# Two recurrent attention layers and their dense layers on one core: late values computed groups ahead, the last quarter of heads in two halves, weights on one queue, and a planner with an urgency per kind of operation

## The chip, the cores and the metric

The kernel runs on one core of one Trainium2 chip. The metric is the device time of one execution in microseconds (us), lower is better. The median of 3 runs of the kernel before is 1724.3 us (1722.43 to 1724.99). The times of the profiled executions are spans of the trace, about 1.8 us shorter than the time of the same run, except for e9 and e17 below: their kept traces span 1725.4 and 1672.1 us, where the profiled run on record took 1727.4 and 1668.4 us, so they show another execution.

## The reference

Two layers are applied in turn, twice: a recurrent attention with memory, then a dense layer. Cut to what matters:

```python
def A(x, mem, Wq, Wk, Wv, Wo):           # 64 segments of 32 tokens, one after the other
    for s in range(64):
        h = concat([mem, x[32*s : 32*s+32]])          # 8 memory rows + 32 tokens = 40 rows
        q, k, v = h @ Wq, h @ Wk, h @ Wv              # 32 heads of 128
        p = softmax(mask(q @ k.T / sqrt(128)))        # 40 x 40 for each head
        o = (p @ v) @ Wo                              # sum over the heads, 40 x 512
        mem = o[:8]                                   # the next segment waits for this
        outs.append(o[8:])

def B(x, w1, w2): return relu(x @ w1) @ w2            # 512 -> 1376 -> 512

x = x + A(layernorm(x)); x = x + B(layernorm(x))      # layer 1
x = x + A(layernorm(x)); x = x + B(layernorm(x))      # layer 2, same weights
```

x is 2048 x 512 in bf16. The memory makes a segment wait for the one before it: q and k, scores, softmax, the transposition of P, attend, projection, and then the memory rows for the next q and k.

## The kernel before: the parts that matter

All weights lie in on-chip memory. Both layers run at once, layer 2 four segments behind layer 1. I call the work on segment k of layer 1 and segment k-4 of layer 2 "step" k; there are 68 steps. What one step does has a fixed list of operations, and a planner in Python fixes at build time in which order each engine runs them. It simulates the engines with a cost for each operation, takes the operation of highest priority among those that can start, computes from the plan how late each operation may start, makes that the new priority, and repeats; the best of 60 randomly varied passes is used.

```python
# the planner, before (cut)
for n in range(PASSES):                                     # 60
    if n > 5:
        look, stay = best[3:]
        look, stay = abs(look + rnd.gauss(0, 0.05)), abs(stay + rnd.gauss(0, 0.2))
    total = self.forward(prio, look, stay)                  # list scheduling, gives an order
    late = self.backward(total)                             # latest starts become priorities
    ...
```

An operation can be bound to one engine, or be offered to two (`copy_op`: ACT or DVE). A matmul uses the full array or half of it (`tile=COL64`, two halves then run side by side).

Each step has four quarters of 8 heads:

```python
for p in range(4):
    qk = [queries_keys(k, hg, a_lo, a_hi) for hg in (2 * p, 2 * p + 1)]
    PTs.append(scores(k, p, a_lo, a_hi, qk))
for p in range(4):
    attend(k, p, a_lo, a_hi, PTs[p])
project(k, act, seg)
```

`scores` is a chain: products (PE), then mask, maximum, subtract (DVE), exp (ACT), sum, reciprocal (DVE), P = e * 1/sum (POOL), transposition (PE), and two copies of the transposed P, rows 0 to 63 and rows 64 to 127 of one PSUM bank, to `PT`, each on ACT or DVE:

```python
for b in range(2):
    def keep(eng, b=b):
        R = slice(64 * b, 64 * b + 64)
        copy_on(eng, PT[R, a_lo:a_hi, :, b, :]..., tp[R, ...]...)
    copy_op(n, keep, r=[tp, "zero PT"], w=[PT, (PT, b)] if b == 0 else [(PT, b)])
```

The values v = h @ Wv are computed in the step for the second half of layer 1's tokens and all of layer 2 (`vw`). The values of the first 16 tokens of each layer-1 segment do not depend on the memory: they are computed for a group of four segments at once (I call them "late values"; four pieces of 8 half-array matmuls of 512 columns), in the step before the group starts, and copied by DMA into place for each segment:

```python
def late_values(g):
    ...                                            # gather x of 4 segments into XG
    values(XG[:, :, :], vg, "vg", ["XG"])          # 4 pieces, PE 0.86 us each
...
if 0 in seg and seg[0] % GS == GS - 1 and seg[0] // GS + 1 < NG:
    late_values(seg[0] // GS + 1)                  # just before it is needed
```

The weights arrive in 1 MB pieces, in pairs on two queues (SP's and POOL's), w1 and w2 right behind them:

```python
pairs = (("q0", "k0"), ("q1", "k1"), ("v0", "v1"), ("q2", "k2"), ("v2", "v3"), ("q3", "k3"), ("o0", "o1"), ("o2", "o3"))
for i, pair in enumerate(pairs):
    for (c, pc), (eng, q) in zip(pair, ((SP, nc.sync), (POOL, nc.gpsimd))):
        ...
```

## Time and profile before

| | before |
|---|---|
| time, median of 3 runs | 1724.3 us |
| PE busy | 95% of the span |
| step 1 starts at | 68.9 us |
| four-step period in the middle | 25.4, 24.2, 25.9, 24.7 us |

How to read it. "PE busy" says little here, because a matmul's record is longer than its spacing (a product of 80 columns is recorded as 0.20 us long, and the next one starts 0.036 us later), so that the records cover short waits. I use another measure all through this document. The "floor" of a stretch is what its matmuls take at the best spacing that the trace shows: 36 ns from start to start for 80 columns, 25 ns for 40 (half of each where two half arrays run side by side), 108 ns for one of 512 columns in half-array pairs, plus 96 ns for every change between full and half array (408 of them). The rest of the stretch is "idle". Before: floor 1584.4 us and idle 138.1 us, of it 50.3 us until step 1 starts, 6.4 us in steps 1 to 3, 15.4 us in steps 4 to 19, 53.1 us in steps 20 to 63, and 12.9 us at the end.

The floor rests on spacings that fit the Trainium skill, "TensorE: Matmul & The Clock Gate", section "Back-to-back issue gap": its isolated gap of N/2.4 + 2.5 ns is 35.8 ns for 80 columns and 216 ns for 512, and this trace shows 36 ns and 216 ns per pair. The same section's sustained figure for matmuls with weight loads, 81 ns at 128 columns, is not what this kernel shows: each of its 80-column products has its own weight load and they still follow each other at 36 ns.

From the page of the kernel before, parts 1, 2 and 4 (busy time by engine; granted PE clock and DMA rate in 40 slices of the span; the chain of waits by engine):

```profile
PE 1632.0 (95%) x40536; PEld 1402.1 (81%) x40536; DVE 909.6 (53%) x2294; ACT 1096.3 (64%) x2657; POOL 357.8 (21%) x873
PEclk8799999999999999999999999999999999999999
GB/s 352 132 22 18 19 18 22 16 21 19 17 20 18 22 18 20 19 18 20 18 22 17 20 19 18 19 18 22 18 19 20 17 16 18 20 15 18 17 6 6
PE 86%; DVE 4%; ACT 3%; SPq 2%; POOL 1%; DMA 1%; issue 1%; ACTq 0%; POOLq 0%; DVEq 0%
```

The work is PE's, but the first slice shows the load of the weights and a lowered clock. The chain of waits of the kernel before, from 25 to 75 us (start, length, what):

```profile
25.59 17.23 SPq L365
...
42.86 15.53 DMA w_sb<-in_B_w_dram
...
59.89 2.13 DMA V_88<-vw
...
66.48 2.15 PE st_124 L876 x64
...
68.65 0.20 DVE HT_80 L892
...
68.89 0.69 PE work_122 L732 x16
```

SP's sequencer sits on the issue of Wo until 42.8 us, the load of w1/w2 takes the engines until 58.4 us, and V's pieces queue up behind it, so that the first step's attention ends, and step 1 starts, at 68.9 us.

One four-step period of the kernel before (steps 32 to 35), as busy time of each engine in each step; the columns are PE, PEld, DVE, ACT, POOL (with instructions), granted PE clock, share of DMA, GB/s:

```profile
830.70:856.10 25.40, 23.45 (x599) 20.93 (x598) 12.78 (x32) 16.37 (x38) 5.47 (x14) 1.00 0.08 19
856.10:880.30 24.20, 23.89 (x601) 20.75 (x598) 13.92 (x34) 17.40 (x43) 6.01 (x14) 1.00 0.10 25
880.30:906.20 25.90, 25.84 (x628) 22.25 (x629) 13.58 (x34) 16.64 (x39) 4.44 (x10) 1.00 0.08 17
906.20:930.90 24.70, 24.70 (x602) 20.59 (x599) 14.45 (x34) 16.22 (x39) 5.40 (x13) 1.00 0.07 16
```

The first step of the four has a floor of 22.4 us and loses 3.0 us. Why is seen in the timeline of its last 10 us (start, length, engine, line, operation, and in brackets the idle time before it and what ended it):

```profile
846.11 0.23 PE L849 MATMUL work_122<-PT_102,V_88 128*64 128x80 bf16 x2 [0.98 <-ACT PT_102 L640]
...
848.77 0.42 ACT L640 CAST PT_103<-work_121 64x320 bf16<-64x320 f32 x1 [0.32 <-PE work_121 L481]
849.22 0.49 DVE L642 CAST PT_103<-work_121 64x320 bf16<-64x320 f32 x1 [0.37 <-ACT PT_103 L640]
849.77 0.20 PE L849 MATMUL work_122<-PT_103,V_88 128*128 128x80 bf16 x1
...
850.10 0.99 POOL L814 TENSOR_TENSOR P_85<-es_101,sm_110 128x160 bf16<-128x160 f32 x2 [1.01 <-DVE sm_110 L798]
...
851.15 0.32 PE L481 MATMUL work_123<-ident,P_85 128*128 128x80 bf16 x4 [0.33 <-POOL P_85 L814]
```

The last quarter's P takes POOL 0.99 us, its transposition waits for that, and the two copies of a transposed P run one after the other (DVE waited for ACT's). The largest wait, 1.2 us from start to start less the floor, ends at 846.11 us, in the first line shown: attend waits there for the PT of an earlier quarter, whose second copy, on ACT, also came after the first.

### The profile page before, as it was taken

To read this page: it belongs to the slowest core of one execution; us is meant where nothing else is said; L and a number is where in the kernel's file an instruction comes from. 1 tells how busy PE (TensorE), PEld (TensorE's weight loads), DVE (VectorE), ACT (ScalarE), POOL (GpSimd) and SP (SyncE) were. 2 spreads that over 40 slices of the span, in tenths; PEclk is the share of its full clock that TensorE was granted. 3 is DMA by queue.
4 is the path that set the end of the run, shared out by engine and by line. 5 is a ranking of instruction groups with operands and counts; after the bars stand their busy time and mean duration, and the time that the engine had idled before them with its cause. 6 is when DMAs were issued, how large, how long until landed. Compare 5 with 4: busy or idle time off the path is not lost.

```text
span 1722.5 us, 89836 instructions
## 1 busy us (share of the span) xinstructions
PE 1632.0 (95%) x40536; PEld 1402.1 (81%) x40536; DVE 909.6 (53%) x2294; ACT 1096.3 (64%) x2657; POOL 357.8 (21%) x873
## 2 busy tenths in 40 slices
PE   2699999999999999999999999999999999999998
PEld 2578888888888888888888888888888888888886
DVE  4345556555555655555565555556555555554554
ACT  1366666666666666666666666666666666666664
POOL 3121222122112212221222222122212212211211
PEclk8799999999999999999999999999999999999999
DMA  9400000000000000000000000000000000000000
GB/s 352 132 22 18 19 18 22 16 21 19 17 20 18 22 18 20 19 18 20 18 22 17 20 19 18 19 18 22 18 19 20 17 16 18 20 15 18 17 6 6
DMA packets 31008, 50.54 MB, mean 29 GB/s; under 512 B 8248, under 2 KB 14400, under 8 KB 30624
## 3 DMA queue, kind: packets, MB, share of 16 engines
q1 hardware_dynamic: 27632, 34.54, 7.9%
q0 software_dynamic: 2560, 9.80, 1.5%
q8 instruction: 317, 5.19, 1.3%
q10 hardware_dynamic: 432, 0.47, 0.1%
q14 instruction: 67, 0.55, 0.1%
HBM read 21.70 MB, written 2.10 MB: 14 GB/s over the span
## 4 chain that ended last, share of the span: by engine, by line
PE 86%; DVE 4%; ACT 3%; SPq 2%; POOL 1%; DMA 1%; issue 1%; ACTq 0%; POOLq 0%; DVEq 0%
PE st_124 L876 15%; PE fill_125 L684 8%; PE fill_126 L684 7%; PE work_122 L732 7%; PE work_120 L732 7%; PE work_123 L732 7%; PE work_119 L732 7%; PE work_121 L732 7%; PE fill_125 L481 6%; PE fill_126 L481 4%; SPq L365 1%; SPq L368 1%; POOL P_85 L814 1%; DMA w_sb<-in_B_w_dram 1%; PE work_119 L759 1%
## 5 line engine op out<-in xcount | busy, mean ns | idle before, releaser
L732 PEld LDWEIGHTS <-Wq_sb 128*128 128x128 bf16 x8704 | 336.0, 100 | 32.8 <-issue 19.1
L876 PE MATMUL st_124<-OT,Wo_sb 128*128 128x80 bf16 (+1 forms) x8704 | 345.7, 200 | 0.7 <-ACT OT L640 0.6
L732 PEld LDWEIGHTS <-Wk_sb 128*128 128x128 bf16 x8704 | 336.0, 100 | 1.3 <-issue 0.8
L876 PEld LDWEIGHTS <-Wo_sb 128*128 128x128 bf16 x8704 | 319.1, 100 | 10.8 <-issue 6.8
L814 POOL TENSOR_TENSOR P_82<-es_100,sm_107 128x160 bf16<-128x160 f32 (+1 forms) x136 | 57.2, 442 | 758.3 <-ACT qT_93 L640 299.5
L849 PEld LDWEIGHTS <-V_88 128*64 128x64 bf16 (+1 forms) x1488 | 89.6, 107 | 45.1 <-issue 34.6
L640 ACT CAST vw<-fill_125 128x512 bf16<-128x512 f32 x134 | 78.0, 582 | 61.8 <-PE fill_125 L684 61.7
L640 ACT CAST vw<-fill_126 128x512 bf16<-128x512 f32 x132 | 76.9, 583 | 49.3 <-PE fill_126 L684 49.2
L481 PEld LDWEIGHTS <-w_sb 128*128 128x128 bf16 (+2 forms) x1752 | 89.7, 104 | 5.3 <-issue 4.8
L814 POOL TENSOR_TENSOR P_84<-es_100,sm_109 128x160 bf16<-128x160 f32 (+1 forms) x136 | 61.8, 476 | 135.8 <-DVE sm_109 L798 103.4
L773 DVE TENSOR_TENSOR es_100<-work_121,maskb 128x320 f32<-128x320 f32 (+1 forms) x38 | 18.5, 487 | 133.7 <-PE work_121 L759 133.7
L684 PEld LDWEIGHTS <-HT_79 128*64 128x64 bf16 x1088 | 55.0, 110 | 39.6 <-issue 0.7
L849 PEld LDWEIGHTS <-vw 128*64 128x64 bf16 (+1 forms) x1480 | 82.1, 106 | 5.6 <-issue 1.9
L481 PE MATMUL fill_125<-w_sb,hT_118 128*64 128x512 bf16 (+1 forms) x645 | 85.8, 380 | 0.0
L684 PEld LDWEIGHTS <-HT_80 128*64 128x64 bf16 x1088 | 54.1, 110 | 37.8
L814 POOL TENSOR_TENSOR P_85<-es_101,sm_110 128x160 bf16<-128x160 f32 (+1 forms) x136 | 59.1, 455 | 112.2 <-DVE sm_110 L798 95.7
L773 DVE TENSOR_TENSOR es_100<-work_119,maskb 128x320 f32<-128x320 f32 (+1 forms) x37 | 17.4, 469 | 122.3 <-PE work_119 L759 118.1
L792 ACT ACTIVATE es_100<-es_100 128x320 f32<-128x320 f32 (+1 forms) x136 | 61.9, 455 | 24.6 <-DVE es_100 L786 22.4
L684 PE MATMUL fill_125<-Wv_sb,HT_79 128*64 128x512 bf16 x560 | 72.9, 382 | 0.2 <-ACT vg L640 0.2
L684 PE MATMUL fill_126<-Wv_sb,HT_80 128*64 128x512 bf16 x560 | 72.3, 380 | 0.0
L814 POOL TENSOR_TENSOR P_83<-es_101,sm_108 128x160 bf16<-128x160 f32 (+1 forms) x136 | 59.3, 458 | 49.0 <-DVE sm_108 L798 45.7
L684 PE MATMUL fill_125<-Wv_sb,HT_80 128*64 128x512 bf16 x528 | 68.2, 380 | 0.0
(364 smaller groups left out, 3902.3 us busy)
## 6 DMA issues: line engine op xcount, KB each, us to landing
V_88<-vw SPq DMA_DIRECT2D x252, 48.0 KB
V_88<-vg SPq DMA_DIRECT2D x252, 32.0 KB
Wq_sb<-in_A_Wq_dram SPq DMA_DIRECT2D x4, 1024.0 KB
Wk_sb<-in_A_Wk_dram POOLq DMA_DIRECT2D x4, 1024.0 KB, 16.2
Wv_sb<-in_A_Wv_dram SPq DMA_DIRECT2D x2, 1024.0 KB
Wv_sb<-in_A_Wv_dram POOLq DMA_DIRECT2D x2, 1024.0 KB, 18.9
Wo_sb<-in_A_Wo_dram POOLq DMA_DIRECT2D x2, 1024.0 KB, 32.6
Wo_sb<-in_A_Wo_dram SPq DMA_DIRECT2D x2, 1024.0 KB
```

What stands on the lines that cost most here:

```text
L365: q.dma_start(out=Wo_sb[:, hs, :], in_=A_Wo.rearrange("h e d -> e h d")[:, hs, :])
L368: q.dma_start(out=W_s[c][:, :, cs], in_=W_v[c][:, :, cs])
L481: nc.tensor.matmul(out_[u:v, :], lhsT=lhsT[:, u:v], rhs=rhs, start=start, stop=stop, tile_position=(0, u))
L640: nc.scalar.copy(out=out_, in_=in_)
L684: nc.tensor.matmul(vp[64 * b:64 * b + 64, :], lhsT=cols[:, c4, :], rhs=Wv_sb[:, c4, n * 512:(n + 1) * 512], start=(c4 == 0), stop=(c4 == N ...
L732: nc.tensor.matmul(qp[:, hi * 2 * L:hi * 2 * L + n], lhsT=W_sb[:, c4, h * Dh:(h + 1) * Dh], rhs=HT[:, c4, c0:c1], start=(c4 == 0), stop=(c ...
L759: nc.tensor.matmul(v[64 * g2:64 * g2 + L, a, b, ii, :], lhsT=qT[:, hi, a * L:(a + 1) * L], rhs=kT[:, hi, a * L:(a + 1) * L], start=True, s ...
L773: nc.vector.tensor_tensor(out=esv(), in0=spv(), op=ALU.add, in1=maskb[:, a_lo:a_hi, :].unsqueeze(2).to_broadcast([128, na, 4, L]))
L792: nc.scalar.activation(out=e, in_=e, func=ACTF.Exp, scale=SCALE)
L814: nc.gpsimd.tensor_tensor(out=o, in0=e, in1=s.unsqueeze(3).to_broadcast([128, na, 2, L]), op=ALU.mult)
L849: nc.tensor.matmul(o[u:u + cols, :, a, :], lhsT=V[:, p, hh * Dh + u:hh * Dh + u + cols], rhs=PT[:, a, hh, :, :], start=True, stop=True, ti ...
L876: nc.tensor.matmul(wo[:, 2 * W * c4 + c0:2 * W * c4 + c1], lhsT=Wo_sb[:, h, c4 * 128:(c4 + 1) * 128], rhs=OT[:, h, c0:c1], start=(h == 0 a ...
```

## The change

Its intent: (1) all weights on one queue (POOL's) in 2 MB pieces, v first, w1/w2 held back; (2) late values computed groups ahead and kept in HBM, groups 1 to 4 while the weights still load, in the space of w1/w2; the layernormed x too; (3) the last quarter of heads split into two halves, so that the recurrence's last softmax is half as long, and P's product offered to POOL or DVE; (4) the planner: three passes, no random search, a table of urgencies, and a rule for work that is spare. The core of the diff:

```diff
+UNITS = ((0, (0, 1)), (1, (0, 1)), (2, (0, 1)), (3, (0,)), (3, (1,)))
-PASSES = 60
+PASSES = 3
+RULE = (0.045, 0.734, 51.008, 20.581)
+AHEAD = {
+    "attend.ev": 0.03, "attend.mm": -1.07, "dense_layer.mm": -0.93, ...
+    "scores.keep": -13.15, "scores.mul": -5.63, "scores.total": 20.81, "values.mm*": -37.11, ...
+}
 ...
+            t, o = min((c for c in starts if c[0] <= lo + look), key=rank)
+            if e == PE and o.spare:
+                soon = [c for c in starts if t < c[0] < t + o.cost and prio[c[1].seq] < prio[o.seq] - far]
+                if soon: ...                       # leave the slot to the one that is due soon
 ...
-        pairs = (("q0", "k0"), ("q1", "k1"), ("v0", "v1"), ...)
+        for i, part in enumerate(("v0", "v2", "q0", "k0", "q2", "k2", "o0", "o2")):
+            ...                                    # 2 MB each, all on nc.gpsimd
+    def prepare_group(g):
+        ...                                        # load x, layernorm, xh[g] to HBM
+        late_values(g, xnT)
-        values(XG[:, :, :], vg, "vg", ["XG"])
+        if 1 <= g <= EARLY:
+            room = (w1_sb, w2_sb)[(g - 1) // 2][:] ...
+        values(XG[:, :, :], room, name, ["XG"])
+        def put():
+            nc.sync.dma_start(out=vh[g][:], in_=room[:, :, :])
+        plan.op(SP, 0.78, put, r=["loaded", ...], w=[("vh", g)], lag=4.0)
 ...
-            plan.op(POOL, t_pool(n // 2), mul, r=[es, sm], w=[("P", p, b)])
+            plan.op((POOL, DVE), (t_pool(2 * na * L), t_dve(2 * na * L)), mul, r=[es, sm],
+                    w=[("P", p, b, x) for b in range(b0, b1) for x in xs])
 ...
+    for g in range(1, NG):
+        prepare_group(g)
+    load_dense()
-        for p in range(4):
-            qk = [queries_keys(k, hg, a_lo, a_hi) for hg in (2 * p, 2 * p + 1)]
-            PTs.append(scores(k, p, a_lo, a_hi, qk))
+        for p, xs in UNITS:
+            heads = heads_of(p, xs)
+            qk = [queries_keys(k, p, heads[j:j + 4], a_lo, a_hi) for j in range(0, len(heads), 4)]
+            PTs.append(scores(k, p, xs, a_lo, a_hi, qk))
```

"loaded" is a time in the planner's picture.

## The prediction

> **What bounds it.** TensorE: matmuls cover 95% of the span (page, part 1); the chain of waits is 86% PE. I split PE time into a "floor" (every matmul at the best spacing the trace shows: 36 ns for 80 columns, 25 ns for 40, 216 ns for 512, 108 ns each where two half arrays run together, plus 96 ns for each change between full and half array) and the rest, "idle". Before: floor 1584 us (408 changes, 39 us of it) and idle 138 us. Idle by part, from the PE timeline: 50 us until step 1 starts at 68.9 us; 6 us in steps 1-3; 69 us in steps 4-63; 13 us in the last four steps and the tail.
>
> **Startup.** Windows 0-25 and 25-50 us show 346 and 352 GB/s: loading weights is the limit. Wo's issue sits in the queue until 42.9 us, w1/w2 follow, and step 0's attention waits for V0 pieces queued behind them (V_88<-vw landed at about 62 us), so Wo's last product ends at 68.6 us. The change puts the attention weights, v first, on one queue and holds w1/w2 back: 16.8 MB at 352 GB/s is 48 us, so an estimate of step 1 starting at 52-54 us. The Trainium skill, "DMA: Bandwidth & Descriptors", "Issuing engines are not separate DMA queues", says that DMAs from any engine run on the same 16 engines (so one queue should lose none; this trace, with two, cannot confirm it). Meanwhile PE computes early groups' late values: by the instruction order, floor before step 1 grows from 18.6 to 34.5 us. Idle there falls from 50 to about 18 us. Cold clock (0.60 and 0.72 granted at 25-75 us) may cost 2-4 us.
>
> **Steady state.** The old plan has four-step periods: steps of floor 22.4, 23.6, 25.4, 24.6 us take 25.4, 24.2, 25.9, 24.7. The first, without late values, loses 3.0 us to the recurrence (last scores, softmax, turn, attend, project, memory). Splitting the last quarter halves the last softmax's operations (VectorE about 0.49 to 0.32 us each, six in a chain) and lets projection overlap it, about 1 us shorter. Late values become filler, mostly spent by step 20. By the new order, steps 24-63 have floors of 23.3 and 22.9 us alternately, with at most about 0.5 us uncovered (projection followed directly by q/k). I estimate 0.4 us idle per step: 6 us in steps 4-19, 18 us in 20-63, against 69 us.
>
> **Cost.** Changes of array mode rise from 408 to 490, +8 us; matmul work is unchanged. VectorE gains 800 instructions (half of P's products move from POOL, halves split), +100 us of 910: it stays near 60%, off the path.
>
> **Sum.** Floor 1592 + idle 18 + 6 (steps 1-3) + 6 + 18 + 12 (end) = 1652; with some slip, 1655 us, 4% less. Range 1638-1682. Chances: faster by over 2% 0.93, within 2% 0.06, slower 0.01.
>
> **Signs.** Step 1's first q/k at 52-55 us (before 68.9). PE busy share 97% or more. Steps 24-63 take 23.3-23.8 us; steps 4-19 about 25.5. Attend's 1 us waits for PT disappear. VectorE busy about 1000 us, POOL about 240-260.
>
> **What would make it wrong.** One software queue loading slower than 352 GB/s (step 1 at 58 us or later); the recurrence still setting steps 24-63, now without late values as filler, at 24 us or more (each 0.5 us per step is 20 us); VectorE delaying evictions so that PE waits for PSUM banks; V0's late part from HBM coming late on the SP queue.

## The result

The changed kernel takes 1681.44 us (median of 4 runs, 1681.01 to 1684.49), against 1723.81 us of the kernel before in the same rounds. The ratio is 0.9758, 95% interval 0.9741 to 0.9775. The change is 2.4% faster; predicted was 4.0%. From the page after:

```profile
PE 1632.9 (97%) x40522; PEld 1396.9 (83%) x40522; DVE 1070.6 (64%) x3095; ACT 1062.2 (63%) x2665; POOL 246.6 (15%) x608
PEclk9999999999999999999999999999999999999999
GB/s 358 214 81 35 39 37 28 37 35 37 34 39 16 39 28 17 26 21 24 17 26 20 19 21 19 27 17 25 18 27 16 19 24 21 18 18 18 18 5 6
PE 81%; DVE 12%; DMA 3%; issue 2%; POOL 1%; ACT 1%; POOLq 0%; ACTq 0%; DVEq 0%
```

PE's share rose as foretold, but DVE's part of the chain rose from 4% to 12%. The sum of the prediction against the trace, all in us:

| | before | predicted | after |
|---|---|---|---|
| floor (changes of array mode) | 1584.4 (408) | 1592 (490) | 1592.3 (490) |
| idle until step 1 | 50.3 | 18 | 28.6 |
| idle in steps 1 to 3 | 6.4 | 6 | 6.0 |
| idle in steps 4 to 19 | 15.4 | 6 | 5.6 |
| idle in steps 20 to 63 | 53.1 | 18 | 35.7 |
| idle in steps 64 to 67 and after | 12.9 | 12 | 11.4 |
| sum | 1722.5 | 1652 | 1679.6 |

Two terms are off, by 10.6 and 17.7 us, and they are the whole miss. First the start. The chain of waits after, from 40 to 66 us:

```profile
8.90 48.50 DMA Wo_sb<-in_A_Wo_dram
...
57.45 0.97 PE st_161 L951 x32
58.42 0.98 PE fill_162 L757 x8
59.41 0.50 PE st_161 L951 x16
...
62.38 0.86 PE fill_163 L757 x8
63.24 0.50 PE work_156 L809 x16
```

The last half of Wo lands at 57.4 us, not at about 50; four pieces of late values (fill) and the last projections stand after it. The traffic of the first 60 us in the changed kernel, by queue (packets, MB, share of the 16 engines' time), and two of its transfers:

```profile
q0 software_dynamic: 4224, 16.78, 74.9%
q1 hardware_dynamic: 1120, 2.61, 12.0%
q10 hardware_dynamic: 1520, 1.52, 7.7%
...
vh_92<-w_sb SPq DMA_DIRECT2D x1, 512.0 KB
```

The weights are q0's 16.78 MB. Besides them 4.1 MB (3.4 MB until Wo had landed) ran on SP's and ACT's queues: late values on their way to HBM, x, layernormed x, pieces of V. From the packets: while q0 was nearly alone (5 to 20 us) it moved 1.9 to 2.05 MB in each 5 us; from 25 us on, with the others, 1.3 to 1.8.

Then the steady state. Steps 40 to 43 of the changed kernel, columns as before:

```profile
1019.10:1042.70 23.60, 23.57 (x613) 21.51 (x614) 14.21 (x43) 16.77 (x41) 2.23 (x5) 1.00 0.07 18
1042.70:1067.00 24.30, 23.67 (x586) 19.88 (x584) 16.86 (x45) 14.53 (x38) 4.27 (x10) 1.00 0.12 30
1067.00:1090.50 23.50, 23.50 (x612) 21.47 (x613) 14.22 (x43) 16.67 (x41) 2.22 (x5) 1.00 0.08 18
1090.50:1114.80 24.30, 23.72 (x586) 19.95 (x583) 16.76 (x45) 14.51 (x37) 4.21 (x10) 1.00 0.07 19
```

Even steps take 23.55 us with 0.25 us idle, odd steps 24.31 us, although their floor is the smaller one (22.87): they lose 1.44 us. The end of an odd step in the changed kernel:

```profile
1063.55 0.69 DVE L685 TENSOR_TENSOR ob_74<-xg_70,fill_162 64x512 bf16<-64x512 f32 x1
...
1064.27 0.32 DVE L703 CAST PT_139<-work_156 64x160 bf16<-64x160 f32 x1
...
1064.62 0.29 ACT L701 CAST PT_139<-work_156 64x160 bf16<-64x160 f32 x1 [0.81 <-DVE PT_139 L703]
1064.96 0.20 PE L924 MATMUL work_160<-PT_139,V_123 128*128 128x80 bf16 x1 [0.26 <-ACT PT_139 L701]
...
1066.70 0.22 DVE L967 CAST HT_80<-st_161 128x64 bf16<-128x64 f32 x1 [0.72 <-PE st_161 L951]
...
1066.98 0.71 PE L809 MATMUL work_159<-HT_80,Wq_sb 128*128 128x80 bf16 x15 [0.32 <-DVE HT_80 L967]
```

Two waits are seen. Attend waits 0.43 us (start to start, less the floor) for PT: its first copy stood behind a residual sum of 0.69 us on DVE, and its second copy, on ACT, waited for the first. And the next step's first q waits 0.48 us for the copy of the memory columns (HT_80), with no other matmul between. One more, of 0.2 us, is among the scores. (Lines of busy time hide all this: PE's record shows 23.67 us busy there.)

### The profile page after: what moved, and what is told of

Its sections match the earlier page's. It is cut to its first block, busy times and chain, and to the rows that moved or that the text cites. A ratio compares the mean times of both kernels' runs of the same rounds, so it can differ in the third digit from the quotient of the medians.

```text
span 1679.6 us, 90364 instructions
## 1 busy us (share of the span) xinstructions
PE 1632.9 (97%) x40522; PEld 1396.9 (83%) x40522; DVE 1070.6 (64%) x3095; ACT 1062.2 (63%) x2665; POOL 246.6 (15%) x608
## 4 chain that ended last, share of the span: by engine, by line
PE 81%; DVE 12%; DMA 3%; issue 2%; POOL 1%; ACT 1%; POOLq 0%; ACTq 0%; DVEq 0%
PE st_161 L951 13%; PE fill_162 L757 8%; PE fill_163 L757 8%; PE work_159 L809 7%; PE work_157 L809 7%; PE work_156 L809 7%; PE work_160 L809 7%; PE work_158 L809 6%; PE fill_163 L514 5%; PE fill_162 L514 4%; DMA Wo_sb<-in_A_Wo_dram 3%; DVE OT L703 2%; DVE ob_74 L685 1%; DVE ln_147 L522 1%; POOL P_85 L886 1%
## 5 line engine op out<-in xcount | busy, mean ns | idle before, releaser
L951 PE MATMUL st_161<-OT,Wo_sb 128*128 128x80 bf16 (+1 forms) x8704 | 354.5, 200 | 2.9 <-DMA Wo_sb<-in_A_Wo_dram 2.9
L951 PEld LDWEIGHTS <-Wo_sb 128*128 128x128 bf16 x8704 | 322.5, 100 | 24.3 <-issue 18.2
L701 ACT CAST vw<-fill_162 128x512 bf16<-128x512 f32 x115 | 67.3, 585 | 56.7 <-PE fill_162 L757 52.8
L701 ACT CAST vw<-fill_163 128x512 bf16<-128x512 f32 x103 | 60.3, 585 | 47.6 <-PE fill_163 L757 43.7
L924 PEld LDWEIGHTS <-V_123 128*64 128x64 bf16 (+1 forms) x1526 | 86.2, 107 | 4.0 <-issue 0.6
L514 PEld LDWEIGHTS <-w_sb 128*128 128x128 bf16 (+1 forms) x1496 | 86.8, 100 | 0.8 <-DVE ob_74 L685 0.5
L757 PEld LDWEIGHTS <-HT_80 128*64 128x64 bf16 x1088 | 51.3, 111 | 32.5 <-issue 2.5
L860 ACT ACTIVATE es_136<-es_136 128x320 f32<-128x320 f32 (+2 forms) x170 | 68.8, 405 | 14.0 <-DVE es_136 L856 9.6
L860 ACT ACTIVATE es_135<-es_135 128x320 f32<-128x320 f32 (+2 forms) x170 | 68.6, 403 | 14.2 <-DVE es_135 L856 6.2
L757 PEld LDWEIGHTS <-HT_81 128*64 128x64 bf16 x1088 | 51.0, 110 | 30.9 <-issue 1.0
L757 PE MATMUL fill_162<-Wv_sb,HT_81 128*64 128x512 bf16 x584 | 76.4, 384 | 0.0
L757 PE MATMUL fill_163<-Wv_sb,HT_80 128*64 128x512 bf16 x544 | 71.9, 387 | 0.0
L757 PE MATMUL fill_162<-Wv_sb,HT_80 128*64 128x512 bf16 x544 | 71.4, 385 | 0.0
L856 DVE TENSOR_TENSOR es_136<-es_136,mx_141 128x320 f32<-128x320 f32 (+2 forms) x170 | 68.9, 405 | 1.0
L853 DVE TENSOR_REDUCE mx_141<-es_136 128x8 f32<-128x320 f32 (+2 forms) x170 | 67.7, 398 | 1.8
L856 DVE TENSOR_TENSOR es_135<-es_135,mx_140 128x320 f32<-128x320 f32 (+2 forms) x170 | 68.0, 400 | 0.9
L853 DVE TENSOR_REDUCE mx_140<-es_135 128x8 f32<-128x320 f32 (+2 forms) x170 | 67.7, 398 | 1.4
L757 PE MATMUL fill_163<-Wv_sb,HT_81 128*64 128x512 bf16 x504 | 66.3, 385 | 0.0
L514 PE MATMUL fill_163<-w_sb,hT_155 128*64 128x512 bf16 (+3 forms) x376 | 54.4, 380 | 0.0
```

The costliest lines, as they stand in the source:

```text
L514: nc.tensor.matmul(out_[u:v, :], lhsT=lhsT[:, u:v], rhs=rhs, start=start, stop=stop, tile_position=(0, u))
L701: nc.scalar.copy(out=out_, in_=in_)
L757: nc.tensor.matmul(vp[64 * b:64 * b + 64, :], lhsT=cols[:, c4, :], rhs=Wv_sb[:, c4, n * 512:(n + 1) * 512], start=(c4 == 0), stop=(c4 == N ...
L853: nc.vector.tensor_reduce(out=mx[:, As], in_=es3(), axis=AX.X, op=ALU.max)
L856: nc.vector.tensor_tensor(out=es3(), in0=es3(), op=ALU.subtract, in1=mx[:, As].unsqueeze(2).to_broadcast([128, ns * na, L]))
L860: nc.scalar.activation(out=es[:, A], in_=es[:, A], func=ACTF.Exp, scale=SCALE)
```

## Experiments

Every kernel but one gave the reference's result by intent; that one is marked. "Idle" is the span less the floor of the built order. In some traces up to 9 us of matmul records are missing, so idle by step is an upper bound there, marked "at most".

| run | what it is | median us | ratio to before (95%) | idle until step 1 | idle steps 20-63 |
|---|---|---|---|---|---|
| changed kernel | | 1681.4 | 0.9758 (0.9741-0.9775) | 28.6 | 35.7 |
| e1_hold_stores | other traffic waits for Wo | 1701.5 | 0.9869 (0.9854-0.9884) | at most 48.6 | at most 37 |
| e5_early_norm | zeroing in pieces | 1680.6 | 0.9746 (0.9732-0.9761) | at most 27 | at most 38 |
| e6_stores_behind | stores behind the weights | 1682.4 | 0.9755 (0.9740-0.9769) | 26.6 | 38.4 |
| e12_add_later | one sum later on DVE | 1676.7 | 0.9726 (0.9711-0.9740) | 30.1 | 29.1 |
| e17_memory_aside | e12, no wait for the memory | 1669.9 | 0.9686 (0.9672-0.9701) | 29.2 | 27.0 |
| e14_behind_norm_add | e5, e6 and e12 together | 1668.1 | 0.9671 (0.9657-0.9686) | at most 23 | at most 29 |
| e3_spread | late values released over the steps | 1696.0 | 0.9842 (0.9824-0.9860) | at most 28 | at most 42 |
| e4_unsplit | last quarter whole | 1770.7 | 1.0271 (1.0252-1.0290) | at most 31 | at most 113 |
| e7_no_urgency | empty table | 1723.4 | 0.9989 (0.9972-1.0006) | at most 30 | at most 59 |
| e8_old_planner | old planner | 1695.4 | 0.9837 (0.9821-0.9854) | 26.6 | 36.5 |
| e9_serial_keeps | planner told of serial copies | 1727.0 | 1.0012 (0.9995-1.0029) | 30.5 | 54.3 |
| e10_old_unsplit | old planner, unsplit | 1764.6 | 1.0236 (1.0220-1.0251) | 27.7 | 119.3 |
| e15_old_spread | old planner, spread | 1714.3 | 0.9941 (0.9926-0.9956) | 28 | about 49 |
| e16_old_unsplit_spread | old planner, unsplit, spread | 1725.4 | 1.0006 (0.9991-1.0021) | 29 | 71 |

### The start

**e1_hold_stores.** SP's transfers wait for a small DMA that reads the end of Wo.

```diff
+        def gate():
+            nc.sync.dma_start(out=held[:], in_=Wo_sb[0:1, H - 1, 0:8])
+        plan.op(SP, 0.5, gate, r=[("W", "o", 2)], w=["loaded"], lag=0.0)
```

> Edit to the changed kernel: the first instruction of the SP queue is a 16-byte copy of the last Wo values to HBM, so that every SP transfer (the stores of late values, 0.5 MB each, and the x loads of groups 5 and 6) really waits until Wo has landed, as the planner believed it did. PE order unchanged (floor 1592 us, 490 mode changes). Theory A (in the changed kernel's trace about 1.7 MB of SP traffic lands before Wo, the weights' queue falls from 2.0 to 1.3-1.5 MB per 5 us): Wo lands about 4 us earlier, at 53 us instead of 57; step 1 starts at 58-60 instead of 63.2; whole kernel 2 to 4 us faster than the changed kernel, 1678 us. Rival B (one software queue is slower by itself late in the load, or HBM is): Wo lands at 57 as before, step 1 at 63, whole kernel the same or slower.

Wo landed at 51.6 us instead of 57.4, with 1.0 MB of other traffic before it instead of 3.4, and with the weights' queue at 1.5 to 2.05 MB in each 5 us: the other traffic does cost the load 6 us. (Not the whole fall of the rate is company, though: from 40 to 50 us the queue was alone in this run and still moved only 1.75 and 1.51 MB in 5 us. Why is open.) But step 1 started at 83.2 us. The waits of this run up to 90 us (who, for what: us in total, times, longest):

```profile
ACT vg L707 <- DMA held<-Wo_sb: 27.8, 1, 27.8
...
PE work L844 <- ACT kT L707: 26.1, 2, 25.9
```

ACT, which has nothing to do with the gate, waited 27.8 us for the gate's DMA. In the built program ACT's next DMA raises the same semaphore as the gate's DMA (one of eight that SP's and ACT's DMAs are given) and waits first until the gate's has landed. So the whole-kernel answer is spoilt; the landing of Wo is the answer that stands.

**e5_early_norm.** DVE's zeroing of 9 us, which held back the first layernorm, is cut into single operations.

```diff
-        plan.op(DVE, 9.5, zero_rest, w=["zero PT"] + ... + ["zero x"] + ...)
+        plan.op(DVE, 0.3, zero(p_xr.tiles), w=["zero xr"])
+        plan.op(DVE, 0.9, zero([vw]), w=[...])
+        ...                                        # one operation for each tile
```

> Edit to the changed kernel: the 9 us of zeroing on VectorE ahead of group 0's layernorm is cut into single operations, so that the planner can put the normalisation first. Theory: TensorE idles 15.2 us at the start because of VectorE, not of the weights (Wv's first part lands at about 8-9 us): with the normalisation early, the first value product starts at 9 to 11 us, the late values of groups 1-4 are done before Wo lands, step 1 starts at 59 to 61 us, and the whole is 2 to 5 us faster, near 1678. Rival: Wo's landing at 57 us alone sets step 1; the early start only moves idle time from before 15 us to between 20 and 57: step 1 at 62-63 us, the whole the same within 1 us.

PE's first values started at 10.9 us instead of 15.2, step 1 at 61.5 us instead of 63.2, and the time is the same within its interval. Wo was issued later in this order (its second half at 13.3 us instead of 8.9) and landed at 57.9 us. Of the 4.3 us that PE gained at its first values, longer waits before step 1 took back 2.7 (for Wq, for Wo, and for the copies of x to XG).

**e6_stores_behind.** The stores of groups 0 to 4 go to the weights' queue, behind them.

```diff
-            nc.sync.dma_start(out=vh[g][:], in_=room[:, :, :])
+            (nc.gpsimd if early else nc.sync).dma_start(out=vh[g][:], in_=room[:, :, :])
```

> Only the stores of the first five groups' late values move: onto the queue of the weights, behind them. Theory (the store traffic of 0.5 MB each slowed the weights, and that is the 10.7 us by which the start was longer than predicted): Wo lands at about 53 us instead of 57, step 1 starts at about 59 us instead of 63, the whole is 2 to 4 us shorter (ratio to the kernel before about 0.974). Rival (the fixed order, with its late-value pieces between the last products, and the cold clock set the start, not the load): step 1 moves by less than 1.5 us and the whole by less than 1 us.

Step 1 started at 60.1 us, idle until there 26.6 us: a part of the theory. Wo's second half landed 46.5 us after its issue instead of 48.5. The whole did not get shorter: steps 4 to 63 idle 5 us more than in the changed kernel's trace. With the planner's new order the gain was given back; by which wait is not settled. Start times also scatter: e12, whose order is the same up to step 1, started it at 64.6 us instead of 63.2. So 1 to 2 us at the start in one trace prove nothing by themselves.

### The odd steps

**e12_add_later.** The order of the changed kernel, with one edit after planning: DVE's last residual sum of a pair goes behind the copy of the last PT and the layernorm. (By the built program this moved 23 of the 32 sums, those of all odd steps from 19 to 61 and of step 65; the other nine did not stand right before that pair. The expectation speaks of 32.)

```diff
-        for o in plan.order():
+        for o in add_later(plan.order()):      # moves add1 and its store behind [scores.keep, layernorm.norm]
```

> The planner's order is kept except that in 32 pairs of segments VectorE does the last residual sum (0.69 us) after the copy of the last transposed P and the layernorm instead of before them. Theory (0.43 us of the 1.44 us that an odd step loses is this sum standing before the copy that attend waits for): odd steps 24.31 -> 23.9 us, idle 1.44 -> about 1.0, the whole about 8 us shorter (1672 to 1675 us). Rival (the wait comes back at the next link of the chain, at the copies of OT, of the layernormed x or of the memory): odd steps stay at 24.1 to 24.3, the whole moves by under 3 us.

Odd steps took 23.93 us instead of 24.31, their idle fell from 1.44 to 1.06 us, even steps stayed at 23.55: the theory, for the steps. The whole is 4.8 us shorter (median 1676.7), not 8: steps 20 to 63 gave 6.6 us, and step 4 started 3.8 us later in this trace, with nothing changed before it but chance. The end of an odd step in this run:

```profile
1064.15 0.32 DVE L722 CAST PT<-work 64x160 bf16<-64x160 f32 x1
...
1064.50 0.29 ACT L720 CAST PT<-work 64x160 bf16<-64x160 f32 x1
...
1065.12 0.20 PE L943 MATMUL work<-PT,V 128*128 128x80 bf16 x1
...
1067.19 0.28 PE L828 MATMUL work<-HT,Wq_sb 128*128 128x80 bf16 x3 [0.32 <-DVE HT L986]
```

PT's copies are no longer late (attend follows a projection without a wait), and the wait for the memory columns is as it was.

**e17_memory_aside.** As e12, and from step 8 on the memory columns are written to a tile that no product reads. This computes a wrong recurrence; the comparison still passed, so with these inputs the memory weighs less than its tolerance.

```diff
-                nc.vector.tensor_copy(out=HTn[:, :, m_lo:m_hi], in_=v(2 * W)[:, :, m_lo:m_hi])
+                if k < 8: nc.vector.tensor_copy(out=HTn[:, :, m_lo:m_hi], in_=v(2 * W)[:, :, m_lo:m_hi])
+                else:     nc.vector.tensor_copy(out=mem0T[:], in_=v(2 * W)[:, :, m_lo:m_lo + M])
```

> A wrong result on purpose: the order of the run with the residual sum after the copy (1676.7 us, odd steps 23.91 us), but from step 8 on VectorE writes the memory columns to a tile that no q/k product reads, so the first product of a step needs not wait for them. Theory (the memory copy is the last wait at the end of odd steps, 0.48 us): odd steps 23.91 -> 23.4 to 23.5 us, even steps unchanged at 23.55, the whole 1663 to 1668 us. Rival (behind it stands the copy of the layernormed x on POOL or the eviction of q and k): odd steps stay above 23.7 us, the whole above 1672 us.

Odd steps took 23.77 us, 0.15 less and not 0.48: the rival, as named. The end of an odd step in this run:

```profile
1061.32 0.69 DVE L704 TENSOR_TENSOR ob<-xg,fill 64x512 bf16<-64x512 f32 x1
...
1062.05 0.42 DVE L722 CAST xnB<-fill 128x256 bf16<-128x256 f32 x1
...
1062.60 0.52 POOL L738 COPY HT<-xnB 128x128 bf16<-128x128 bf16 x2 [1.90 <-DVE xnB L722]
...
1062.94 0.73 PE L828 MATMUL work<-HT,Wq_sb 128*128 128x80 bf16 x16 [0.16 <-POOL HT L738]
```

Now the first q waits for the layernormed x that POOL copies, and that copy is late because the moved sum stands before the xnB copy on DVE. Two chains end almost together here; taking one away shows the other. (The time of 1669.9 us lies between the two expectations, 6.7 us below e12's. The traces differ by 4.9 us: 2.4 us until step 4, where nothing was edited, 2.1 us in steps 20 to 63, 0.4 us elsewhere. Both kept traces are of executions longer than the median of their kernel, e17's of one 3.7 us longer than its profiled run on record, so the time of the whole can't be divided up more finely.)

**e9_serial_keeps.** The planner is told that the second copy of PT follows the first.

```diff
-            copy_op(n, keep, r=[tp, "zero PT"], ...)
+            copy_op(n, keep, r=[tp, "zero PT", *([(PT, 0)] if b else [])], ...)
```

> The changed kernel, but the planner is told that the second copy of transposed P starts after the first; urgencies as they are. Floor 1607.8 us (652 changes of array mode against 490). Theory (the planner's picture of two copies side by side is what leaves the waits): idle in steps 20 to 63 at most 15 us, the whole at most 1675 us. Rival (urgencies tuned for one picture do not fit another, as with the unsplit quarter): the whole 1690 us or more.

The rival: 1727.0 us, with 652 changes of array mode (floor 1607.8 us) and 54 us idle in steps 20 to 63. A truer picture of the built program gave a worse order. That the table of urgencies, made for the other picture, is the reason is likely but not shown: the edit was not tried with the old planner, nor with an empty table. Whether a table made for the true picture would win is open.

### Which part carries the gain

**e8_old_planner, e4_unsplit, e10_old_unsplit** cross the planner and the split, with the rest of the change kept; **e7_no_urgency** empties the table.

```diff
 e8:   class Plan: forward(), order() and PASSES = 60 as before
 e4:  -UNITS = ((0, (0, 1)), (1, (0, 1)), (2, (0, 1)), (3, (0,)), (3, (1,)))
      +UNITS = ((0, (0, 1)), (1, (0, 1)), (2, (0, 1)), (3, (0, 1)))
 e10:  both
 e7:  -AHEAD = { ... }
      +AHEAD = {}
```

> The changed kernel with the old planner (60 random passes, no urgencies, no rule for spare work), everything else kept. Its order has a floor of 1603 us (602 changes of array mode against 490), 11 us more. Theory (the split and the late values done early shorten the recurrence whatever the planner): idle in steps 20 to 63 at most 1.0 us per step, so the whole is about 1603 + 29 + 12 + 44 + 12 = 1700 us or less. Rival (split and urgencies work only together): idle 2 us or more per step there, the whole 1740 us or more, slower than before.

> Edit to the changed kernel: the last quarter of heads is one unit again, all else kept (planner, urgencies, early late values, weights on one queue). Floor 1586 us, 420 mode changes (70 fewer than the changed kernel, 6.7 us). If the split shortens the recurrence by about 1 us per step as I predicted: steps without late values take 24.2 us or more again (floor 24.0 and 22.0), idle in steps 20-59 rises from 35 us to 50-70, and the whole is 10 to 25 us slower than the changed kernel, 1690 to 1706. Rival: the planner with its urgencies, not the split, made the gain: the whole is within 6 us of the changed kernel or faster by the saved mode changes.

> The old planner and the last quarter of heads whole, while the late values stay early and the weights stay on one queue: those two parts of the change alone. Floor 1579 us (348 changes of array mode). Theory (without the split the recurrence sets the steps without late values, as the first step of four did before, 3 us each): idle in steps 20 to 63 about 2 to 3 us per step, step 1 at about 63 us, the whole 1715 to 1750 us. Rival (the old planner can cover the recurrence without the split): idle 0.7 us per step or less, the whole about 1579 + 29 + 12 + 31 + 12 = 1663 us, faster than the changed kernel.

> The changed kernel with the new planner, but every kind of operation with the same urgency (floor 1596 us, 526 changes of array mode). Theory (the table only polishes an order that split and passes already give): idle in steps 20 to 63 below 55 us, the whole 1685 to 1705 us, about as with the old planner. Rival (the table carries the gain, its rule alone is worse than the old random search): the whole 1720 us or more.

| median us | last quarter whole | split |
|---|---|---|
| old planner | 1764.6 | 1695.4 |
| new planner with its table | 1770.7 | 1681.4 |
| new planner, empty table | not run | 1723.4 |

e8: the theory, 1695.4 us and 0.83 us idle per step. e10: its theory in direction, and more: 1764.6 us, above the range expected. Two steps of each, first e10 (with a stretch of 3.4 us inside the even step as the second line), then e8:

```profile
857.50:884.10 26.60, 24.71 (x606) 22.56 (x607) 13.33 (x36) 16.35 (x38) 2.94 (x6) 0.94 0.07 15
875.30:878.70 3.40, 3.35 (x51) 3.35 (x51) 1.87 (x5) 1.76 (x6) 0.55 (x1) 0.50 0.02 5
884.10:908.60 24.50, 23.82 (x597) 20.57 (x594) 14.58 (x34) 16.47 (x39) 4.28 (x10) 1.00 0.11 30
```

```profile
835.70:860.10 24.40, 24.03 (x601) 21.50 (x601) 14.39 (x41) 16.86 (x42) 3.15 (x7) 1.00 0.09 22
860.10:884.50 24.40, 23.93 (x587) 20.29 (x586) 15.30 (x43) 16.32 (x41) 3.96 (x9) 1.00 0.11 28
```

Unsplit, the even step loses about 4.1 us (26.6 us on a floor of 22.4); split it takes 24.4. Of the 4.1 us only 2.6 are waits. The other 1.6 us are slower matmuls: from 875.3 to 878.7 us the granted clock is 0.50, and 80-column products follow each other at 67 ns instead of 36. The trace of e10 has such a stretch of 3.4 us in each of the 22 even steps from 20 to 63, that of e4 in 15 of the 22 odd steps (there the odd steps are the long ones); the kernel before, the changed kernel and e8 have none there. So in steps 20 to 63 e10's idle of 119 us is 86 us of waits (gaps of over 0.13 us beyond the floor) and 33 us of slower matmuls, e8's 36.5 us is 32 and 4. The stretches come in the steps with long waits; whether the waits bring them about was not tested.

So the split is worth 69 us under the old planner and 89 us under the new one. The new planner with its table is worth 14 us on top of the split, and without the split nothing (6 us slower; the table had been made for the split kernel). e7 says what in the planner is worth it: with the table empty the kernel is as slow as the kernel before, 28 us behind the old random search. By time the rival held there, and the table carries the planner's gain (the theory's other half was right: with the floor of the built order idle in steps 20 to 63 is 54 us).

**e3_spread, e15_old_spread, e16_old_unsplit_spread** undo "groups ahead" for most groups: the pieces of late values are released one by one over the steps (e3: groups 7 to 15, one piece in 1.5 steps, new planner; e15 and e16: groups 5 to 15, one piece in each step from 12 to 55, old planner; e16 unsplit as well).

```diff
+FREE, FROM, EVERY = 6, 4, 1.5                 # e15, e16: 4, 12, 1
-        values(XG[:, :, :], room, name, ["XG"])
+        values(XG[:, :, :], room, name, ["XG", *([("go", opens(g, p)) for p in ps] if g > FREE else [])], ps)
+    def opens(g, p): return FROM + int(EVERY * (4 * (g - FREE - 1) + p))
 # ("go", k + 1) is written by step k's copy of the memory columns
```

> Edit to the changed kernel: late values of groups 7 to 15 may not run before a given step (one 0.87 us chunk every 1.5 steps, from step 4 to step 56), instead of all being spent by step 22. Floor 1597 us, 538 mode changes (+4.6 us). Theory F (steps 23-59 lose 1.44 us in every second step because no filler is left; steps 4-18, with filler, lose 0.14 and 0.35): idle in steps 23-59 falls from about 31 us to about 12, and the whole is 10 to 15 us faster than the changed kernel, near 1668. Rival R (those waits come from where the order puts projection, attend and q/k in odd steps, and filler does not sit in them; a chunk of 0.87 us is longer than the 0.43 and 0.48 us gaps): idle in odd steps stays at 1 us or more, whole within 5 us of the changed kernel or slower by the extra mode changes, 1680 to 1686.

> Old planner and split as in the run that took 1695.4 us, but the late values of groups 5 to 15 are released one piece per step in steps 12 to 55 instead of early (floor 1597 us, 540 changes of array mode against 1603 and 602). Theory (with the split the recurrence no longer needs filler, so early late values cost nothing and the spread gains only its smaller floor): idle in steps 20 to 63 stays at 30 to 40 us, the whole 1685 to 1698 us. Rival (filler in every step covers what is left): idle there falls to 15 us or less, the whole 1675 us or less, and the early late values were a mistake.

> Old planner, last quarter whole, late values released over steps 12 to 55: of the change only the weights' queue and the early work of the first groups stay (floor 1577 us, 326 changes). Theory (unsplit, early late values had taken the filler away from the recurrence, which is why that run took 1764.6 us): idle in steps 4 to 63 falls from 136 us to 60 to 75 us as in the kernel before, step 1 at about 62 us, the whole 1690 to 1705 us. Rival (the loss in that run came from something else in the changed kernel, such as the copies' engines or the loads of V from HBM): idle stays above 110 us, the whole above 1735 us.

e3 was slower by 15 us than the changed kernel: odd steps still idled 0.9 to 2.2 us (1.6 on average), and the floor grew by 5 us (538 changes of mode). e15 was slower by 19 us than e8, and both of its expectations missed: spread pieces neither cost nothing nor filled gaps. Inside that run, steps with a piece (32 to 35) idle 1.1 us on average, those without (58 to 61) 0.7 us, so a piece costs its 0.87 us and lengthens the waits; which wait it lengthens is not settled. (Of the 19 us, 9 are idle time in steps 4 to 19, where e8 has most of its late values.) e16 answers the other way: unsplit, spreading wins 39 us (1764.6 to 1725.4), idle in steps 4 to 63 falls from 136 to 96 us. That is the theory's direction, not its size (60 to 75 us were expected). And little of it is wait: the waits of steps 4 to 63 fall from 99 to 87 us, the slower matmuls from 37 to 9, for in steps 20 to 63 e16 has only three of the stretches at half the granted clock.

Read together (the releases of e15 and e16 are a timetable of mine, not quite what the kernel before does): without the split, taking the late values out of the steps cost 39 us, about 12 of them in longer waits and 28 in matmuls at a lower granted clock; with the split taking them out gains 19 us. That the late values were filler which covered the recurrence explains the waits; the clock's part is seen, but not explained, by these runs. So the parts of the change are not independent: weights, queue and early groups alone (e16) leave the time where it was, for the 21 us gained at the start are lost again later.

### The mends together

**e14_behind_norm_add** puts e5, e6 and e12 together.

> The three small mends together: stores of the early groups behind the weights, VectorE's zeroing in single pieces so that the first layernorm comes early, and the last residual sum after the copy that attend waits for. If they add: step 1 at 58 to 60 us, odd steps 23.9 us, the whole 1671 to 1676 us (ratio about 0.970). If the start is set by the order of PE's late-value pieces and the cold clock, it is as with the last of them alone, 1676 to 1678 us.

It takes 1668.1 us (ratio 0.9671), faster than both kernels and than the range expected, 13.3 us below the changed kernel. Step 1 starts at 57.3 us, with 23 us idle before it instead of 28.6. Odd steps take 23.93 us as in e12. Alone, e5 and e6 did not shorten the whole, although their traces started step 1 earlier, by 1.7 and 3.1 us; e14's start is 5.9 us earlier, little more than the sum. So it is not shown that the two remove two limits of one wait (PE's late begin, Wo's late landing) and need each other. What e6 gained was lost again after step 4, and in e14 it was not; e5 and e6 were not run together without e12.

## Why the prediction was wrong, and where it was right

1. **Floor: right.** 1592 us and 490 changes predicted, 1592.3 and 490 measured. The instruction order, known before the run, gives this part exactly.
2. **Start: direction right, size wrong.** The prediction's step: "16.8 MB at 352 GB/s is 48 us, so an estimate of step 1 starting at 52-54 us", and "Idle there falls from 50 to about 18 us". Step 1 started at 63.2 us, idle 28.6 us. The rate was not too high (403 to 416 GB/s in the windows of 5 to 25 us); the bytes were too few. 4.1 MB of other traffic (3.4 MB until Wo had landed) shares the engines, at least 3 MB of the 4.1 brought by the change itself (four stores of 0.5 MB of late values, and 128 KB each for the x and layernormed x of the early groups), and e1 shows its price: with 1.0 MB of it instead of 3.4 Wo lands at 51.6 us. I had quoted the Trainium skill, "DMA: Bandwidth & Descriptors", section "Issuing engines are not separate DMA queues", for the harmless half of it (one queue loses nothing) and had not applied it to the stores: transfers from any engine interleave on the same 16 engines. The traces agree with both halves: 1.9 to 2.05 MB per 5 us on one queue nearly alone, 1.3 to 1.8 in company. The rest of the 28.6 us, from the trace: 3.5 us before PE's first instruction, about 11 us until the first values at 15.2 us (behind DVE's zeroing), 8.9 us in six waits, 7.8 us of them for weights, and 5.6 us of slow spacing: from 15.2 to 19.5 us and from 30 to 33 us, for instance, a pair of 512-column matmuls took 427 ns instead of 216. (The granted clock was 0.67 from 30 to 35 us, but is recorded as 1.00 from 15 to 20 us.) For slow spacing I had "2-4 us". e14 wins back 5.5 us of this term.
3. **Steps 4 to 19: right** (6 predicted, 5.6 measured).
4. **Steps 20 to 63: the term was mis-sized, 18 predicted and 35.7 measured.** The prediction's step: "with at most about 0.5 us uncovered (projection followed directly by q/k). I estimate 0.4 us idle per step". The 0.48 us after the projection is there as foretold, in odd steps alone. Not foreseen was that the odd steps lose 1 us more: 0.38 us from a residual sum that the order puts before the copy of PT (shown by e12), the rest in waits among the scores, the layernorm and the copies, which the trace shows and no run here removed. I had listed "the recurrence still setting steps 24-63 ... at 24 us or more" as what would make it wrong, and that is what the odd steps do. My reading of the order looked for stretches of PE without filler; it did not look at what stood before the chain's links on DVE.
5. **The split: right in direction, and worth far more than I had put down for it.** I had "about 1 us shorter" for the first step of four (and expected 10 to 25 us in e4). With late values moved away the split is worth 69 to 89 us, 1.0 to 1.3 us in each of 68 steps; and with all the rest of the change but without it the kernel is 2.7% slower than before (e4). In steps 20 to 63 of the traces under the old planner 54 us of it are shorter waits, as I had argued, and 29 us are matmuls that no longer fall into stretches at half the granted clock, which I had not thought of; against that the split's order has 24 us more floor over the whole kernel.
6. **The sum of the signs.** Right: PE 97%; even steps 23.55 us; steps 4 to 19 at 25.5 us on average (24.3 and 26.6 in turn); POOL 246.6 us. Wrong: step 1 at 52-55 us; odd steps at 23.3-23.8 us; the waits of attend for PT, which shrank to 0.43 us and did not disappear; VectorE at 1070.6 us and not 1000.

The added idle of points 2 and 4, 10.6 + 17.7 = 28.3 us, less 0.7 us elsewhere, is the difference between 1652 and 1679.6 us. What stays open: the wait that gives e6's gain back, the wait that a spread piece lengthens in e15, what lowers the granted clock in the unsplit runs, and whether the planner with a true picture of PT's copies and a table made for it would win more. Not tested one by one are the single queue, v first and w1/w2 held back, the layernormed x in HBM, and the offer of P's product to DVE, which all runs here keep.

## What to carry to other kernels

When a change moves work to a better time through HBM, count its bytes against whatever else loads at that time, not only the bytes that were there before. When work that filled gaps is taken out of a recurrent loop, the loop's own chain must be shortened in the same change, or the gaps come back larger: here one part without the other costs 39 us and the two together gain. Look at the granted clock of the slow steps before all lost time is called waiting: here 33 of 119 us were slower matmuls. Test small mends of one stage together as well as singly, because a gain of 2 or 3 us at the start can be lost in the rest of a new order, and be kept in another. And a schedule tuned for one picture may have to be tuned again when the picture, even for the better, is changed.

## What the Trainium skill lacked or had wrong

- "TensorEngine Tiling (Array Packing)", section "Key Properties", says that a change of tiling mode drains the engine, without a figure. A change between full and half array costs about 96 ns (start to start, beyond the usual spacing); 490 of them are 47 us of 1680.
- "PSUM — Partial Sum Buffer", section "PSUM bank collisions raise a hardware error", says that accesses to different quadrants of a bank may run at the same time. The two copies of a transposed P read partitions 0 to 63 and 64 to 127 of one bank on two engines, and in the lines shown above, of before and of after, the second starts only when the first has ended (ACT's idle 0.81 us ended with DVE's copy). In the built program the second copy waits for the first one's semaphore; why it is ordered so is not shown. The page gives no figure for what a stricter order costs; here it puts off the second copy by the length of the first, 0.3 to 0.5 us in the lines above. No run here ran them side by side.
- "DMA: Bandwidth & Descriptors", table of properties: about 358 GB/s as the limit of HBM for a core. This core drew 403 to 416 GB/s in 5 us windows from 5 to 25 us while loading. That is below the page's fabric ceiling of 435 GB/s, and "HBM Reference", section "Specifications (TRN2)", does say that a core alone gets more than its share: the table's line misleads only when it is read by itself.
- No page found says that a DMA of one engine can hold up the issue of another engine's DMA by a shared semaphore, as it does in the built program of e1: ACT waited 27.8 us for a transfer that SP had issued.
